# Attention's second product with the values as stationary operand and a transposed result, probabilities normalized first

## The chip, the core and the metric

The kernel runs on one core of a Trainium2 chip. The core has a matrix engine (TensorE, PE in the profile, with its weight loads as PEld), three engines for elementwise work (VectorE or DVE, ScalarE or ACT, GpSimd or POOL) and DMA queues, most of them issued from SyncE (SP). The metric is the device time of one execution in microseconds. Before the change three runs took 991.99, 993.06 and 994.40 us; the median is 993.06.

## The reference

Chunked attention feeds a dense feed-forward layer with squared ReLU, and that feeds a layer of eight experts, of which each token uses one:

```python
for c in range(nc):                       # chunks of 32 queries, 24 per sequence
    q_c = q[:, :, c_start:c_end]
    k_full = concat([mem_k, k[:, :, l_start:r_end]])      # 8 memory rows + 56 keys
    v_full = concat([mem_v, v[:, :, l_start:r_end]])
    scores = scale * q_c @ k_full.T
    a = exp(scores - max(scores))
    a = a / (sum(a) + 1e-09)
    out[:, :, c_start:c_end] = a @ v_full
x = out.transpose(0, 2, 1, 3).reshape(3072, 512)          # 8 heads of 64
x = relu(x @ w_in) ** 2 @ w_out                           # 512 -> 2048 -> 512
...                                                       # top-1 of 8 experts, 512 -> 1024 -> 512
```

All arrays are float32. Attention has 4 batches, 8 heads, 768 tokens and 64 numbers per head, so 3072 tokens in all.

## The kernel before

Tokens come in 24 units of 128, and two units form a block of 256. For each block b a class `Duo` does attention and a class `Block` does the dense layer; later, pairs and slots of tokens sorted by expert go through the experts.

A duo's steps: `scores_mm` multiplies queries by keys (64 products in float32, each with a stationary operand of 64 rows by 32 columns and 64 moving columns; a head pair `hp` has two heads in the two row halves, `par`, and four chunks `c` in four column groups). `scores_max`, `scores_sub` and `scores_exp` make e, with the queries of a unit on the partitions. `norm` sums e over the keys and takes the reciprocal r. `transpose_a` turns e with 8 transposes on TensorE and copies it to `at` on ScalarE. `av` multiplies `at` (stationary, 64 by 32) by the values (64 moving columns), again 64 products, and `av_scale` multiplies the result by r on VectorE into x. `transpose_x` turns x with 8 more transposes, and copies it as a rounded high part xh (ScalarE) and a remainder xl (VectorE), which are the moving operands of the dense layer. All these use one PSUM tile of two banks (tag "a", one buffer); the two row halves of `av` write to different banks (index `par`).

```python
nc.tensor.matmul(
    self.ps[ts][rows, par, n : n + 64],
    lhsT=left[t][half, hp, rows],
    rhs=right[t][half, hp, c, :],
```

The dense layer walks a list `seq` of (block, f), with 16 slices f of the hidden layer. Each step issues `mm1` (12 products of 256 columns and then relu and square on ScalarE and VectorE), then what `todo` planned for this step, then `mm2` of the step two before (6 products of 512 columns). Every engine takes its instructions in the order in which the program wrote them; a step of attention is put into that order by `plan_duo` with step numbers: scores and `norm` at s, `transpose_a` at t, `av` at v, `transpose_x` at x. Before: for duos 3 to 11 these are n+1, n+3, n+4 and n+6, where n is the first step of the block before (plus 3 for duo 4, plus 2 for duo 5). The loads of the next duo's keys and values are planned at x+1 and x+3, and its queries at x+2.

Duos 0 and 1 and the conversion of the first weight tiles (`split_w_...`, four VectorE passes and two ScalarE passes for each tile of w_in or w_out) are written out by hand ahead of that loop. Duo 0 goes through it unit by unit, u0 and u1. `keep_busy(n)` there issues n products whose result nobody reads (spin).

Of the kernel before, what the change touches and what calls it, by code (L numbers as in the profile page):

```python
# [8 lines left out]
F32 = mybir.dt.float32  # L9
# [5 lines left out]
ALU = mybir.AluOpType  # L15
AX = mybir.AxisListType

P = 128
# [8 lines left out]
NU = NT // P  # L27
UPS = 6
# [5 lines left out]
BOTH = (0, 1)  # L34
# [17 lines left out]
def chunk_attention_relu2_moe_top1_kernel(ctx: ExitStack, tc, qk, vv, qt, kv, w_in, w_out, wg, wexp, consts, out):  # L52
    nc = tc.nc
# [5 lines left out]
    ap_ = ctx.enter_context(tc.tile_pool(name="ap", bufs=2))  # L59
# [27 lines left out]

    class Duo:  # L90
        def __init__(self, b):
            self.b = b
            self.units = (2 * b, 2 * b + 1)
            self.first, self.q, self.k, self.v = {}, {}, {}, {}
            self.ps, self.mx, self.r = {}, {}, {}
            self.e = self.at = self.x = None


        def load_first(self, t):
# [87 lines left out]
        def norm(self, ts=BOTH):  # L187
            n = 8 * len(ts)
            sm = sp_.tile([P, n], F32, tag="sm", name=f"sm{self.b}_{ts[0]}")
            e = self.e[:, self.heads(ts)].rearrange("p a b k -> p (a b) k")  # L190
            nc.vector.tensor_reduce(out=sm, in_=e, axis=AX.X, op=ALU.add)
            nc.vector.tensor_scalar_add(sm, sm, EPS)
            self.r[ts] = sp_.tile([P, n // 2, 2], F32, tag="rs", name=f"rs{self.b}_{ts[0]}")
            nc.vector.reciprocal(self.r[ts].rearrange("p a b -> p (a b)"), sm)

        def transpose_a(self):
            self.transpose_a_mm()
# [15 lines left out]
            to = self.at[:, ts[0] : ts[-1] + 1].rearrange("p t a c -> p t (a c)")  # L213
            nc.scalar.copy(to, self.ps[ts][:, : len(ts)])

        def av(self):
            self.av_mm()
            self.av_scale()

        def av_mm(self, ts=BOTH, pool=ps_a, tag="a"):  # L220
            self.banks("psx", ts, pool, tag)
            self.products([self.at[:, 0], self.at[:, 1]], self.v, ts)

        def av_scale(self, ts=BOTH):
            if self.x is None:
                self.x = ap_.tile([P, 8, 2, 64], F32, tag="x", name=f"x{self.b}", bufs=1)
            nc.vector.tensor_tensor(
                self.x[:, self.heads(ts)].rearrange("p a b d -> p b a d"),
                self.by_half(ts),
                self.r[ts].rearrange("p a b -> p b a").unsqueeze(3).to_broadcast([P, 2, 4 * len(ts), 64]),  # L230
                op=ALU.mult,
            )

        def transpose_x(self):
            self.transpose_x_mm()
            self.transpose_x_copy()

        def transpose_x_mm(self, ts=BOTH, pool=ps_a, tag="a"):
            self.transposes("pst", self.x.rearrange("p a b d -> p (a b d)"), ts, pool, tag)

        def transpose_x_copy(self, ts=BOTH):
            self.transpose_x_hi(ts)
            self.transpose_x_lo(ts)

        def transpose_x_parts(self, ts):
            s = slice(ts[0] * P, ts[-1] * P + P)
            hi, lo = (x[:, :, s].rearrange("p k (t c) -> p t k c", c=P) for x in blocks[self.b].parts())
            return hi, lo, self.ps[ts][:, : len(ts)].rearrange("p t (k c) -> p t k c", c=P)

        def transpose_x_hi(self, ts=BOTH):  # L250
            hi, lo, ps = self.transpose_x_parts(ts)
            nc.scalar.copy(hi, ps)

        def transpose_x_lo(self, ts=BOTH):
            hi, lo, ps = self.transpose_x_parts(ts)
            nc.vector.tensor_tensor(lo, ps, hi.bitcast(F32), op=ALU.subtract)


# [522 lines left out]
    def plan(n, fn, *args):  # L781
        todo.setdefault(n, []).append((fn, args))

    def plan_duo(b, s, t, v, x):
        d = duos[b]
        plan(s, d.scores)
        plan(s, d.norm)
        plan(t, d.transpose_a)
        plan(v, d.av)
        plan(x, d.transpose_x)  # L790
        if b + 1 < NB:
            after = duos[b + 1]
            k0, q, k1 = (bits[15] + 1, s + 1, v + 1) if b == 2 else (x + 1, x + 2, x + 3)
            plan(k0, after.load_kv, 0)
            plan(q, after.load_q, 0)
            plan(q, after.load_q, 1)
            plan(k1, after.load_kv, 1)
# [3 lines left out]
    bits = dict(zip(range(3, 16), (2, 4, 6, 8, 10, 12, 14, 15, 17, 18, 20, 21, 23)))  # L801
# [13 lines left out]
    plan(bits[14] + 1, duos[2].load_kv, 1)  # L815
    plan(23, lambda: prepare())
    n = at[0, NF - 2]
    plan_duo(2, n - 3, n - 1, n, n + 2)
    for b in range(3, NB):
        n = at[b - 1, 0] + {4: 3, 5: 2}.get(b, 0)  # L820
        plan_duo(b, n + 1, n + 3, n + 4, n + 6)

    def plan_gate(b, n):
        bl = blocks[b]
# [5 lines left out]
    n = at[2, 7]  # L830
# [31 lines left out]
    for p in range(NP):  # L862
        n = at[NB + p, 0]
# [24 lines left out]
    n = at[NB, 0]  # L888
# [22 lines left out]
    with tc.manual_schedule():  # L911
        nc.gpsimd.memset(ones, 1.0)
        d0, d1 = duos[0], duos[1]
# [4 lines left out]
        def hold(tile_, until):  # L918
            nc.gpsimd.tensor_copy(tile_[0:1, 0:1], until)
# [12 lines left out]
        def keep_busy(n):  # L932
            for _ in range(n):
                nc.tensor.matmul(spin, lhsT=ones, rhs=ones.unsqueeze(1).to_broadcast([P, 4, P]), start=True, stop=True)
# [10 lines left out]
        d1.load_first_v()  # L945
        d0.scores_sub(u0)
        d0.scores_mm(u1, *other)
        d0.scores_exp(u0)
        d0.transpose_a_mm(u0)
        d0.transpose_a_copy(u0)  # L950
        keep_busy(3)
        d0.scores_max(u1)
        d0.scores_sub(u1)
        d0.scores_exp(u1)
        split_w_exp(*i0, a)
        d0.norm(u0)
        d0.av_mm(u0)
        d0.av_scale(u0)
        split_w_shift(*i0, a)
        split_w_or(*i0, a, steps=(0,))  # L960
        d0.transpose_a_mm(u1, *other)
        d0.transpose_a_copy(u1)
        keep_busy(3)
        d0.norm(u1)
        o0t = load_w(*o0, issue=False)
        hold(o0t.bitcast(F32), d0.r[u1][0:1, 0, 0:1])
        load_w(*o0)
        load_w(*i1)
        nc.sync.dma_start(cst[:, P:], consts[:, P:])
        d0.av_mm(u1, *other)  # L970
        d0.av_scale(u1)
        split_w_or(*i0, a, steps=(1,))
        d0.transpose_x_mm(u0)
        d0.transpose_x_hi(u0)
        keep_busy(4)
        d0.transpose_x_lo(u0)
        split_w_hi(*i0, a)
        split_w_lo(*i0, a)
        d0.transpose_x_mm(u1, *other)
        d0.transpose_x_copy(u1)  # L980
        d1.scores_mm()
        split_w_exp(*i0, b)
        b0.mm1_products(0)
        keep_busy(8)
# [3 lines left out]
        d1.scores_exp()  # L988
        split_w_shift(*i0, b)
        split_w_or(*i0, b)  # L990
        d1.transpose_a_mm()
        d1.transpose_a_copy()
        split_w_hi(*i0, b)
        d1.norm()
        split_w_lo(*i0, b)
        keep_busy(3)
        d1.av_mm()
        split_w_exp(*o0)
        b0.mm1_products(1)
        d1.av_scale()  # L1000
        split_w_shift(*o0)
        split_w_or(*o0, steps=(0,))
        d1.transpose_x_mm()
        d1.transpose_x_hi()
        keep_busy(4)
        d1.transpose_x_lo()
        split_w_or(*o0, steps=(1,))
        b0.relu(1)
        b1.mm1_products(0)
# [162 lines left out]
```

## Time and profile before

| | us |
|---|---|
| median of three runs | 993.06 |
| the profiled execution | 993.26 |
| its span, first to last instruction | 991.1 |
| TensorE busy | 966.1 (97%) |
| VectorE busy | 609.2 (61%) |
| ScalarE busy | 458.9 (46%) |
| GpSimd busy | 94.4 (10%) |

The span is what the profiler saw; the profiled execution's own time is 2.2 us longer. Busy time of TensorE counts matrix products whose ends are modelled, so it is not work at its peak. Duos 2 to 11 lie between 104 and 580 us of the span, where the dense layer runs; duos 0 and 1 lie in the first 33 us; the experts follow from about 660 us.

### The profile page before, as it was taken

To read this page: it belongs to the slowest core of one execution; us is meant where nothing else is said; L and a number is where in the kernel's file an instruction comes from. 1 tells how busy PE (TensorE), PEld (TensorE's weight loads), DVE (VectorE), ACT (ScalarE), POOL (GpSimd) and SP (SyncE) were. 2 spreads that over 40 slices of the span, in tenths; PEclk is the share of its full clock that TensorE was granted. 3 is DMA by queue.
4 is the path that set the end of the run, shared out by engine and by line. 5 is a ranking of instruction groups with operands and counts; after the bars stand their busy time and mean duration, and the time that the engine had idled before them with its cause. 6 is when DMAs were issued, how large, how long until landed. Compare 5 with 4: busy or idle time off the path is not lost. (4 is left out here: it accounts for less than half of the span.)

```text
span 991.1 us, 21589 instructions
## 1 busy us (share of the span) xinstructions
PE 966.1 (97%) x8973; PEld 856.3 (86%) x8973; DVE 609.2 (61%) x1133; ACT 458.9 (46%) x808; POOL 94.4 (10%) x92
## 2 busy tenths in 40 slices
PE   7899999989999999999999999999999999999996
PEld 4699898979999999999999998989899999888885
DVE  5989764434545454445453545647776666799995
ACT  3777433223333333333333333534454454688885
POOL 0000000100000000000000001101222221111111
PEclk9999999989999999999999999999999999999999
DMA  8456530220303030302021002663965666464531
GB/s 350 172 194 229 185 116 35 29 102 1 129 1 129 1 129 1 129 2 103 27 74 57 23 2 87 176 215 120 332 252 220 215 227 238 171 227 140 213 120 40
DMA packets 30855, 129.18 MB, mean 130 GB/s; under 512 B 8543, under 2 KB 9055, under 8 KB 18850
## 3 DMA queue, kind: packets, MB, share of 16 engines
q1 hardware_dynamic: 25506, 113.84, 32.0%
q0 software_dynamic: 5248, 13.92, 4.6%
q8 instruction: 72, 1.18, 0.5%
q14 instruction: 29, 0.24, 0.1%
HBM read 142.19 MB, written 13.61 MB: 157 GB/s over the span
## 5 line engine op out<-in xcount | busy, mean ns | idle before, releaser
L346 PE MATMUL ph<-xh,wi 128*128 128x256 f32 x1536 | 285.4, 283 | 3.0 <-ACT wi L305 1.0
L346 PEld LDWEIGHTS ph<-xh,wi 128*128 128x128 f32 x1536 | 252.0, 191 | 20.4 <-ACT wi L305 1.4
L346 PE MATMUL ph<-xl,wi 128*128 128x256 f32 x768 | 217.9, 284 | 4.1 <-issue 4.1
L356 ACT ACTIVATE r<-ph 128x256 f32<-128x256 f32 x192 | 73.3, 382 | 308.1 <-PE ph L346 288.8
L361 DVE TENSOR_TENSOR g<-r 128x256 f32<-128x256 f32 x168 | 70.9, 422 | 223.3 <-ACT r L356 222.2
L376 PE MATMUL py<-wo,gh 128*128 128x512 f32 x384 | 160.3, 417 | 0.0
L377 PE MATMUL py<-wo,gh 128*128 128x512 f32 x384 | 151.8, 395 | 0.0
L378 PE MATMUL py<-wo,gl 128*128 128x512 f32 x384 | 150.9, 393 | 0.0
L346 PEld LDWEIGHTS ph<-xl,wi 128*128 128x128 f32 x768 | 147.0, 191 | 4.3 <-issue 4.3
L613 DVE TENSOR_TENSOR x<-raw,x 128x1024 fp32r<-128x1024 f32 x88 | 103.1, 1222 | 6.7 <-ACT x L612 4.6
L365 DVE TENSOR_TENSOR gl<-g,gh 128x256 fp32r<-128x256 f32 x192 | 81.6, 425 | 24.4 <-ACT gh L363 2.4
L613 DVE TENSOR_TENSOR p<-raw,p 128x1024 fp32r<-128x1024 f32 x64 | 78.2, 1222 | 23.3 <-ACT p L612 22.3
L378 PEld LDWEIGHTS py<-wo,gl 128*128 128x128 f32 x384 | 72.7, 189 | 17.0
L612 ACT CAST x<-raw 128x1024 fp32r<-128x1024 f32 x88 | 87.2, 1055 | 0.0
L470 POOL DMA_INDIRECT listd<-ent,idx x24 | 24.2, 1009 | 630.1 <-DVE idx L468 570.8
L376 PEld LDWEIGHTS py<-wo,gh 128*128 128x128 f32 x384 | 73.1, 190 | 12.8 <-issue 2.2
L363 ACT ACTIVATE gh<-r 128x256 fp32r<-128x256 f32 x192 | 79.8, 416 | 5.3
L377 PEld LDWEIGHTS py<-wo,gh 128*128 128x128 f32 x384 | 73.3, 191 | 8.3
L612 ACT CAST p<-raw 128x1024 fp32r<-128x1024 f32 x64 | 66.6, 1040 | 0.0
L759 PE MATMUL po<-x,ht 128*128 128x512 f32 x264 | 65.5, 397 | 0.6 <-DVE ht L749 0.6
L759 PEld LDWEIGHTS po<-x,ht 128*128 128x128 f32 x264 | 48.1, 188 | 10.2 <-DVE ht L749 1.0
L629 POOL DMA_INDIRECT out<-o,slots x27 | 35.5, 1316 | 216.0 <-DVE o L623 94.5
(217 smaller groups left out, 1356.9 us busy)
## 6 DMA issues: line engine op xcount, KB each, us to landing
raw<-in_wexp SPq DMA_DIRECT2D x82, 1024.0 KB
kv<-in_kv SPq DMA_DIRECT2D x20, 1024.0 KB
raw_o<-in_w_out SPq DMA_DIRECT2D x8, 1024.0 KB
raw_i<-in_w_in SPq DMA_DIRECT2D x7, 1024.0 KB
ydram<-y SPq DMA_DIRECT2D x24, 256.0 KB
q<-in_qt SPq DMA_DIRECT2D x20, 256.0 KB
qk<-in_qk SPq DMA_DIRECT2D x4, 768.0 KB
v<-in_vv SPq DMA_DIRECT2D x2, 1024.0 KB
```

Of the source, the lines that this page charges most:

```text
L346: nc.tensor.matmul(ph, lhsT=w_in_part(w, f, k), rhs=x[:, k, :], start=(n == 0), stop=(n == 11))
L356: nc.scalar.activation(r, ph, ACTF.Relu, scale=WSCALE)
L361: nc.vector.tensor_tensor(g, r, r, op=ALU.mult)
L363: nc.scalar.activation(gh, r, ACTF.Square)
L365: nc.vector.tensor_tensor(gl, g, gh.bitcast(F32), op=ALU.subtract)
L376: nc.tensor.matmul(self.y[t], lhsT=gh[:, s], rhs=w_out_part(wh, f), start=(f == 0), stop=False)
L377: nc.tensor.matmul(self.y[t], lhsT=gh[:, s], rhs=w_out_part(wl, f), start=False, stop=False)
L378: nc.tensor.matmul(self.y[t], lhsT=gl[:, s], rhs=w_out_part(wh, f), start=False, stop=(f == NF - 1))
L612: nc.scalar.copy(w[:, 0], t)
L613: nc.vector.tensor_tensor(w[:, 1], t, w[:, 0].bitcast(F32), op=ALU.subtract)
L629: nc.gpsimd.indirect_dma_start(out=out, out_offset=bass.IndirectOffsetOnAxis(ap=slots[:, c, 0:1].bitcast(U32), axis=0), in_=self.y[t], in_ ...
L759: nc.tensor.matmul(self.po, lhsT=self.ht[:, part, f, :], rhs=w[:, wp, j * D : j * D + D], start=(f == 0 and part == 0 and wp == 0), stop=( ...
```

## The change

`norm` now also multiplies e by r, ahead of `transpose_a`. `av_mm` takes the values of a chunk and head as stationary operand (64 rows by 64 columns) and 32 columns of `at` as moving operand, so that its result already has the head's numbers on the partitions and the tokens along the columns, which is the form that the dense layer reads. `av_scale`, the tile x and the 8 transposes of x are gone; xh and xl are taken from the product's PSUM tile. There are four places in the array for a 64 by 64 operand. A product reads row half `par` and writes partition half `par ^ t`, with t the unit in the duo; for the second unit the host therefore swaps the two heads of each pair (`in_turn`). The bank of the result is now the unit `i`.

The plan has `norm` at its own step m, and no x: for duos 3 to 11 scores n+1, norm n+2, `transpose_a` n+5, `av` n+6. The order by hand at the start is rewritten.

```diff
     def norm(self, ts=BOTH):
...
+            self.r[ts] = sp_.tile([P, n], F32, tag="rs", name=f"rs{self.b}_{ts[0]}")
+            nc.vector.reciprocal(self.r[ts], sm)
+            nc.vector.tensor_tensor(e, e, self.r[ts].unsqueeze(2).to_broadcast([P, n, 64]), op=ALU.mult)
...
+        def av(self, ts=BOTH, pool=ps_a, tag="a"):
+            self.av_mm(ts, pool, tag)
+            self.x_hi(ts)
+            self.x_lo(ts)
 
         def av_mm(self, ts=BOTH, pool=ps_a, tag="a"):
             self.banks("psx", ts, pool, tag)
-            self.products([self.at[:, 0], self.at[:, 1]], self.v, ts)
-
-        def av_scale(self, ts=BOTH):
...
-        def transpose_x_mm(self, ts=BOTH, pool=ps_a, tag="a"):
-            self.transposes("pst", self.x.rearrange("p a b d -> p (a b d)"), ts, pool, tag)
...
+            for hp in range(4):
+                for c in range(4):
+                    for i, t in enumerate(ts):
+                        for par in range(2):
+                            half = slice(64 * par, 64 * par + 64)
+                            to = 64 * (par ^ t)
+                            n = P * hp + 32 * c
+                            nc.tensor.matmul(
+                                self.ps[ts][to : to + 64, i, n : n + 32],
+                                lhsT=self.v[t][half, hp, c, :],
+                                rhs=self.at[half, t, hp, 32 * c : 32 * c + 32],
...
-    def plan_duo(b, s, t, v, x):
+    def plan_duo(b, s, m, t, v):
         d = duos[b]
         plan(s, d.scores)
-        plan(s, d.norm)
+        plan(m, d.norm)
         plan(t, d.transpose_a)
         plan(v, d.av)
-        plan(x, d.transpose_x)
...
-            k0, q, k1 = (bits[15] + 1, s + 1, v + 1) if b == 2 else (x + 1, x + 2, x + 3)
+            k0, q, k1 = (bits[15] + 1, s + 1, v + 1) if b == 2 else (v + 1, v + 2, v + 3)
...
-    plan_duo(2, n - 3, n - 1, n, n + 2)
+    plan_duo(2, n - 3, n - 3, n, n + 1)
...
-        plan_duo(b, n + 1, n + 3, n + 4, n + 6)
+        plan_duo(b, n + 1, n + 2, n + 5, n + 6)
...
         split_w_shift(*i0, b)
         split_w_or(*i0, b)
+        d1.norm()
+        split_w_hi(*i0, b)
         d1.transpose_a_mm()
         d1.transpose_a_copy()
-        split_w_hi(*i0, b)
-        d1.norm()
         split_w_lo(*i0, b)
-        keep_busy(3)
-        d1.av_mm()
         split_w_exp(*o0)
         b0.mm1_products(1)
-        d1.av_scale()
+        d1.av_mm()
+        d1.x_hi()
+        d1.x_lo()
         split_w_shift(*o0)
         split_w_or(*o0, steps=(0,))
-        d1.transpose_x_mm()
-        d1.transpose_x_hi()
         keep_busy(4)
-        d1.transpose_x_lo()
         split_w_or(*o0, steps=(1,))
         b0.relu(1)
         b1.mm1_products(0)
```

In the part of the hand-written order that is left out, for duo 0, `keep_busy(4)` stands ahead of `scores_exp(u0)` and `d1.scores_mm()` is followed by `keep_busy(4)` and then by the first products of the dense layer, where it was followed by these products at once.

VectorE at duo 1 (e_443, psx_0_478, xl_572 are this duo's; ws_o, wo and raw_o belong to the first tile of w_out, wi to the first of w_in), before:

```order
L191 TENSOR_REDUCE sm_0_469<-e_443 128x16
L192 TENSOR_SCALAR sm_0_469<-sm_0_469 128x16
L194 RECIPROCAL rs_0_472<-sm_0_469 128x16
L310 TENSOR_TENSOR wi_344<-ws_i_232,wi_344 128x512
L227 TENSOR_TENSOR x_558<-psx_0_478,rs_0_472 128x2x8x64
L285 TENSOR_SCALAR ws_o_543<-ws_o_543 128x1024
L292 SCALAR_TENSOR_TENSOR ws_o_543<-raw_o_290,ws_o_543 128x1024
L256 TENSOR_TENSOR xl_572<-pst_0_562,xh_571 128x2x4x128
L296 SCALAR_TENSOR_TENSOR ws_o_543<-raw_o_290,ws_o_543 128x1024
L365 TENSOR_TENSOR gl_1_586<-g_1_582,gh_1_584 128x256
```

and of the change (e_436, psx_0_484 and xl_550 are the duo's):

```order
L192 TENSOR_REDUCE sm_0_450<-e_436 128x16
L193 TENSOR_SCALAR sm_0_450<-sm_0_450 128x16
L195 RECIPROCAL rs_0_453<-sm_0_450 128x16
L196 TENSOR_TENSOR e_436<-e_436,rs_0_453 128x1024
L307 TENSOR_TENSOR wi_409<-ws_i_242,wi_409 128x512
L253 TENSOR_TENSOR xl_550<-psx_0_484,xh_549 128x2x4x128
L282 TENSOR_SCALAR ws_o_469<-ws_o_469 128x1024
L289 SCALAR_TENSOR_TENSOR ws_o_469<-raw_o_286,ws_o_469 128x1024
L293 SCALAR_TENSOR_TENSOR ws_o_469<-raw_o_286,ws_o_469 128x1024
L362 TENSOR_TENSOR gl_1_566<-g_1_562,gh_1_564 128x256
```

Before, two passes over the weight tile (L285, L292) stand between the scaling of x and the remainder xl; now xl stands ahead of all three passes over that tile, and behind the multiplication of e only one short pass (wi) is ahead of it.

TensorE at the second product of duo 4 (kv_2125 and kv_2207 hold the values of its two units), before, first the product and then, two steps later, the transposes of x:

```order
L135 MATMUL psx_0_2786<-kv_2125,at_2757 32x64 x32
L135 MATMUL psx_0_2786<-kv_2207,at_2757 32x64 x32
L376 MATMUL py_2564<-wo_790,gh_5_2717 128x512
...
L346 MATMUL ph_9_2886<-xl_2095,wi_982 128x256
L205 MATMUL pst_0_2907<-cst,x_2851 128x128 x8
L376 MATMUL py_2564<-wo_918,gh_7_2782 128x512
```

and of the change, the last four rows of the product and what follows:

```order
L234 MATMUL psx_0_2801<-at_2772,kv_2085 64x32 x2
L234 MATMUL psx_0_2801<-at_2772,kv_2167 64x32 x2
L234 MATMUL psx_0_2801<-at_2772,kv_2085 64x32 x2
L234 MATMUL psx_0_2801<-at_2772,kv_2167 64x32 x2
L373 MATMUL py_2524<-wo_898,gh_7_2732 128x512
L374 MATMUL py_2524<-wo_898,gh_7_2732 128x512
```

The product still counts 64, now with the two units in turn, and stands two steps later; the row of 8 transposes is gone.

## Rows read from the trace of the kernel before

**Rows 1.** The page: engines (busy us, share, instructions); the TensorE instruction queue (packets, MB).
```profile
PE 966.1 (97%) x8973; PEld 856.3 (86%) x8973; DVE 609.2 (61%) x1133; ACT 458.9 (46%) x808; POOL 94.4 (10%) x92
...
q8 instruction: 72, 1.18, 0.5%
```
**Rows 2.** Waits of TensorE: what for, us in total, times, longest.
```profile
PE ph L346 <- issue: 4.1, 1, 4.1
...
PE ph L346 <- ACT wi L305: 1.0, 1, 1.0
...
PE ph L346 <- DVE wi L310: 0.9, 1, 0.9
```
**Rows 3.** Timeline of TensorE at duo 11: start us, length us, instruction, count.
```profile
569.68 0.28 PE L346 MATMUL ph<-xl,wi 128*128 128x256 f32 x1
569.89 1.48 PE L135 MATMUL psx<-kv,at 64*32 64x64 f32 x128
571.31 0.50 PE L376 MATMUL py<-wo,gh 128*128 128x512 f32 x1
571.64 0.39 PE L377 MATMUL py<-wo,gh 128*128 128x512 f32 x1
571.87 0.40 PE L378 MATMUL py<-wo,gl 128*128 128x512 f32 x1
...
576.93 0.28 PE L346 MATMUL ph<-xl,wi 128*128 128x256 f32 x1
577.05 1.04 PE L205 MATMUL pst<-cst,x 128*128 128x128 f32 x8
577.84 0.47 PE L376 MATMUL py<-wo,gh 128*128 128x512 f32 x1
578.16 0.39 PE L377 MATMUL py<-wo,gh 128*128 128x512 f32 x1
```
**Rows 4.** Instructions that write psx: count, shortest, median and longest in ns.
```profile
L135 PE MATMUL psx<-kv,at x1280: 212/216/240, 117.0 to 571.2; 64*32 64x64 f32 x183
```
**Rows 5.** Timeline of VectorE, duo 1 and the first weight tiles; idle time before in brackets.
```profile
22.80 0.42 DVE L365 TENSOR_TENSOR gl<-g,gh 128x256 fp32r<-128x256 f32 x1 [0.25 <-ACT gh L363]
...
24.93 1.21 DVE L191 TENSOR_REDUCE sm<-e 128x16 f32<-128x1024 f32 x1
...
27.73 1.21 DVE L227 TENSOR_TENSOR x<-psx,rs 128x1024 f32<-128x1024 f32 x1
...
31.38 1.23 DVE L256 TENSOR_TENSOR xl<-pst,xh 128x1024 fp32r<-128x1024 f32 x1 [0.53 <-ACT xh L252]
...
33.66 0.42 DVE L365 TENSOR_TENSOR gl<-g,gh 128x256 fp32r<-128x256 f32 x1
...
39.98 1.23 DVE L310 TENSOR_TENSOR wi<-ws_i,wi 128x1024 fp32r<-128x1024 f32 x1 [0.17 <-ACT wi L305]
```
**Rows 6.** Timeline of ScalarE at duo 1.
```profile
30.34 1.01 ACT L252 CAST xh<-pst 128x1024 fp32r<-128x1024 f32 x1 [2.82 <-PE pst L205]
```
**Rows 7.** Timeline of TensorE: work behind its waits.
```profile
18.96 1.00 PE L135 MATMUL pss<-qk 64*32 64x64 f32 x76 [1.77 <-issue]
...
32.00 1.04 PE L934 MATMUL spin<-ones 128*128 128x512 bf16 x4 [1.69 <-issue]
...
41.27 0.38 PE L346 MATMUL ph<-xh,wi 128*128 128x256 f32 x1 [0.88 <-DVE wi L310]
...
204.43 0.58 PE L346 MATMUL ph<-xl,wi 128*128 128x256 f32 x1 [4.12 <-issue]
```
**Rows 8.** Stretches: us, busy us by engine, granted clock of TensorE (1.00 full), DMA share, GB/s.
```profile
202.00:206.00 4.00, 1.57 (x6) 1.47 (x7) 1.06 (x3) 0.30 (x1) 0.00 (x0) 0.55 0.33 119
206.00:210.00 4.00, 4.00 (x19) 3.52 (x18) 0.85 (x2) 0.50 (x2) 0.00 (x0) 0.60 0.01 4
```
**Rows 9.** DMA from 201.9 to 203.2 us by queue: packets, MB, share of 16 engines.
```profile
q8 instruction: 1, 0.02, 5.3%
```
**Rows 10.** Timeline of SyncE's queue: issue of a load of keys and values.
```profile
192.62 0.40 SPq L123 DMA_DIRECT2D kv<-in_kv  x1
```

More of the change, by code (lines that the diff above doesn't have):

```diff
@@ L95, in __init__ @@
             self.ps, self.mx, self.r = {}, {}, {}
-            self.e = self.at = self.x = None
+            self.e = self.at = None
         def load_first(self, t):
@@ L192, in norm @@
             nc.vector.tensor_scalar_add(sm, sm, EPS)
-            self.r[ts] = sp_.tile([P, n // 2, 2], F32, tag="rs", name=f"rs{self.b}_{ts[0]}")
-            nc.vector.reciprocal(self.r[ts].rearrange("p a b -> p (a b)"), sm)
+            self.r[ts] = sp_.tile([P, n], F32, tag="rs", name=f"rs{self.b}_{ts[0]}")
+            nc.vector.reciprocal(self.r[ts], sm)
+            nc.vector.tensor_tensor(e, e, self.r[ts].unsqueeze(2).to_broadcast([P, n, 64]), op=ALU.mult)
         def transpose_a(self):
@@ L214, in transpose_a_copy, with x_parts @@
             nc.scalar.copy(to, self.ps[ts][:, : len(ts)])
-        def av(self):
-            self.av_mm()
-            self.av_scale()
+        def av(self, ts=BOTH, pool=ps_a, tag="a"):
+            self.av_mm(ts, pool, tag)
+            self.x_hi(ts)
+            self.x_lo(ts)
         def av_mm(self, ts=BOTH, pool=ps_a, tag="a"):
             self.banks("psx", ts, pool, tag)
-            self.products([self.at[:, 0], self.at[:, 1]], self.v, ts)
-        def av_scale(self, ts=BOTH):
[L225 to L236, printed above, removed]
-        def transpose_x_mm(self, ts=BOTH, pool=ps_a, tag="a"):
-            self.transposes("pst", self.x.rearrange("p a b d -> p (a b d)"), ts, pool, tag)
[L241 to L245, printed above, removed]
+            for hp in range(4):
[9 more added lines that the diff above has]
+                                rhs=self.at[half, t, hp, 32 * c : 32 * c + 32],
+                                start=True,
+                                stop=True,
+                            )
+        def x_parts(self, ts):
             s = slice(ts[0] * P, ts[-1] * P + P)
@@ L248, in transpose_x_parts, with x_hi, x_lo @@
             return hi, lo, self.ps[ts][:, : len(ts)].rearrange("p t (k c) -> p t k c", c=P)
-        def transpose_x_hi(self, ts=BOTH):
-            hi, lo, ps = self.transpose_x_parts(ts)
+        def x_hi(self, ts=BOTH):
+            hi, lo, ps = self.x_parts(ts)
             nc.scalar.copy(hi, ps)
-        def transpose_x_lo(self, ts=BOTH):
-            hi, lo, ps = self.transpose_x_parts(ts)
+        def x_lo(self, ts=BOTH):
+            hi, lo, ps = self.x_parts(ts)
             nc.vector.tensor_tensor(lo, ps, hi.bitcast(F32), op=ALU.subtract)
@@ L947, in chunk_attention_relu2_moe_top1_kernel @@
         d0.scores_mm(u1, *other)
+        keep_busy(4)
         d0.scores_exp(u0)
+        d0.scores_max(u1)
+        d0.norm(u0)
         d0.transpose_a_mm(u0)
         d0.transpose_a_copy(u0)
-        keep_busy(3)
-        d0.scores_max(u1)
         d0.scores_sub(u1)
         d0.scores_exp(u1)
+        keep_busy(3)
         split_w_exp(*i0, a)
-        d0.norm(u0)
         d0.av_mm(u0)
[L958 to L963, printed above, removed]
+        d0.x_hi(u0)
         d0.norm(u1)
         o0t = load_w(*o0, issue=False)
-        hold(o0t.bitcast(F32), d0.r[u1][0:1, 0, 0:1])
+        hold(o0t.bitcast(F32), d0.r[u1][0:1, 0:1])
         load_w(*o0)
@@ L969, in chunk_attention_relu2_moe_top1_kernel @@
         nc.sync.dma_start(cst[:, P:], consts[:, P:])
+        d0.x_lo(u0)
+        keep_busy(3)
+        d0.transpose_a_mm(u1, *other)
+        d0.transpose_a_copy(u1)
+        split_w_shift(*i0, a)
+        split_w_or(*i0, a)
         d0.av_mm(u1, *other)
[L971 to L974, printed above, removed]
+        d0.x_hi(u1)
+        d1.scores_mm()
         keep_busy(4)
-        d0.transpose_x_lo(u0)
+        d0.x_lo(u1)
         split_w_hi(*i0, a)
         split_w_lo(*i0, a)
-        d0.transpose_x_mm(u1, *other)
-        d0.transpose_x_copy(u1)
-        d1.scores_mm()
         split_w_exp(*i0, b)
@@ L990, in chunk_attention_relu2_moe_top1_kernel @@
         split_w_or(*i0, b)
+        d1.norm()
+        split_w_hi(*i0, b)
         d1.transpose_a_mm()
         d1.transpose_a_copy()
-        split_w_hi(*i0, b)
-        d1.norm()
         split_w_lo(*i0, b)
-        keep_busy(3)
-        d1.av_mm()
         split_w_exp(*o0)
         b0.mm1_products(1)
-        d1.av_scale()
+        d1.av_mm()
+        d1.x_hi()
+        d1.x_lo()
         split_w_shift(*o0)
         split_w_or(*o0, steps=(0,))
-        d1.transpose_x_mm()
-        d1.transpose_x_hi()
         keep_busy(4)
-        d1.transpose_x_lo()
         split_w_or(*o0, steps=(1,))
@@ L1107, with in_turn @@
     B, H, S, DH = q.shape
-    qt = q.reshape(B, 4, 2, UPS, P, DH).transpose(0, 3, 2, 5, 1, 4).reshape(NU, P, 4, P)
+    def in_turn(x):
+        x = x.reshape(NU, 2, 64, *x.shape[4:]).copy()
+        x[1::2] = x[1::2, ::-1]
+        return x.reshape(NU, P, *x.shape[3:])
+    qt = in_turn(q.reshape(B, 4, 2, UPS, P, DH).transpose(0, 3, 2, 5, 1, 4))
     def windows(x, mem):
@@ L1120 @@
         [
-            kwn.transpose(0, 3, 2, 6, 1, 4, 5).reshape(NU, P, 4, 4, 64),
-            vwn.transpose(0, 3, 2, 5, 1, 4, 6).reshape(NU, P, 4, 4, 64),
+            in_turn(kwn.transpose(0, 3, 2, 6, 1, 4, 5)),
+            in_turn(vwn.transpose(0, 3, 2, 5, 1, 4, 6)),
         ],
```

## The prediction

> **What bounds the kernel now.** I began with the page: TensorE is busy for 966.1 of 991.1 us, VectorE for 609.2 [rows 1]. So a saving counts where it shortens TensorE's own queue, and only there. The second view was TensorE's waits: they are few, one of 4.1 us put down to "issue", which means that no engine and no data transfer held it, and two of about 1 us for converted weights (wi) from ScalarE and VectorE [rows 2]. The third was the timeline. In the loop TensorE goes from product to product without a gap, so a step of attention costs what it pushes the next product back [rows 3]. In the first 45 us it is different: VectorE works almost without a pause on duo 1 and the first weight tiles, and TensorE waits for what it delivers [rows 5, 7]. Two stretches thus obey two rules, and I price the change in each apart.
>
> **The loop, duos 2 to 11.** The transposes of x are removed. In duo 11 they begin at 577.05, where the next product would have begun (0.12 us after the one at 576.93), and that product begins at 577.84, 0.79 us later. The one behind it follows after 0.32 where 0.23 is usual [rows 3], which adds 0.09. So 0.88 us for each duo, and 10 duos give -8.8 us. The pattern is the same in all ten.
>
> The second product keeps its 64 instructions, in the trace 128 records since each float32 product runs twice. Before, it takes from 569.89 to 571.31, 1.42 us or 11 ns a record [rows 3]. Eight places of the array share them, so one place spends about 90 ns on a record. Of this the 64 moving columns are one part and the load of 32 stationary columns is another that hides under it. Now there are four places, the moving columns halve and the stationary ones double. What a load costs when nothing hides it can be read twice: the longest psx product, the first, takes 240 ns against 216, 24 ns for 32 columns [rows 4]; and the first dense product behind the small ones takes 0.50 against 0.40 us, some 0.1 us for 128 columns [rows 3]. That is about 0.8 ns a column, so a load of 64 columns is an estimated 50 ns. If each place loads while it multiplies, four places deliver a record each 12.5 to 15 ns, and 128 records take 1.6 to 1.9 us. The low end of the cost is nothing: the run stays at 1.42, if the instructions' supply and not the array sets its pace. Less than that I exclude, since neither the instructions nor moving columns for each place in the array become fewer. The high end is that loads and products share the array by two and not by four: 128 times 27 ns, 3.4 us, +2.0. I take +0.5, by the nearer rows, and 10 duos give +5.0 us.
>
> VectorE and ScalarE do as much as before in the loop: a multiplication of 1024 elements (1.21 us [rows 5]) changes its place and its source. It is hidden: `norm` is planned three steps ahead of the transposes, some 8 us, and VectorE is far from full there. Without that cover each duo would cost TensorE up to those 1.2 us. The later `transpose_a` and `av` only use the steps that `transpose_x` leaves. On SP the loads of keys stay at the same steps (v+1 is what x+1 was); on POOL nothing moves in the loop. Both units' values come free at the product's end and not one after the other, within the same 2 us, and nobody waits for that buffer in this stretch. Together the loop gives -3.8 us.
>
> **The start.** In duo 0 chains get longer, but TensorE is held in duo 1's scores until 18.96 in any case [rows 7], and I count nothing there. In duo 1 the chain counts. Four idle products now stand ahead of the first dense products (four last about 0.9 us [rows 7]), so gl at 22.80 [rows 5], which comes from these, moves to 23.7, and all behind it on VectorE too: the sum to 25.8. From the sum to the scaling 2.80 us passed, with a short wi pass of about 0.55 that now comes later; the multiplication starts at 28.05 and ends at 29.25. Then come 8 transposes (0.8), twelve dense products of 0.12 (1.45), the second product (1.5 to 2.0, with its tail), xh on ScalarE (1.01 [rows 6]). The remainder xl, at 31.38 before, can start at 34.7. Meanwhile VectorE has only the wi pass and then stands idle for some 4.5 us, since the three passes over the first tile of w_out are queued behind xl. Before, two of them (from 27.73 plus scaling to the wait of 0.53 ahead of 31.38, 2.0 us) ran during that wait. So the gl that began 2.28 us behind xl, at 33.66, now begins 4.28 behind it, at 39.0: 5.3 us late. From there VectorE hardly pauses before wi at 39.98, for which TensorE waits at 41.27 [rows 5, 7], so TensorE is as late there and never gets it back, being full afterwards. The transposes saved in duos 0 and 1 lie inside these waits. I take +5.0, between 3.5 (no tail at the second product, some idle time swallowed) and 6.5.
>
> On SP the load behind the next tile waits for the same passes and moves with them; POOL's copy that lets the first w_out load go follows duo 0's reciprocal, which moves by under 1 us.
>
> **The stall at 200 us.** This is the largest single item. TensorE stops for 4.12 us until 204.43 without waiting for anything [rows 7]. Its instructions arrive in 72 packets for 17,946 instructions, about 250 each [rows 1]. I counted in the order of instructions (four for a small float32 product, two for others): the three long stops [rows 7] stand at instruction 706, 1218 and 4547, which leave 194, 194 and 195 when divided by 256. So these are ends of blocks of 256 whose successor has not come. Before the restart one instruction packet arrives, after 201.9 [rows 9], behind a load of keys and values of 1 MB issued at 192.62 [rows 10]. Then the clock is granted at about half until 209.2 (0.55 and 0.60 as means [rows 8]): 4.8 us at half speed cost 2.4. The stop costs 6.5 us in all. By my count the change removes 59 instructions ahead of this place (64 for the transposes of duos 0 to 3, less a few idle products and waits), so the block ends 59 instructions later behind duo 4's scores. A step of the dense layer is 36 instructions and 2.85 us, so TensorE reaches the end 4.4 us later, when the packet that came late before has just come. I take -6.5; the bounds are nothing, if the three timed runs had no such stop or the packet is as late again, and -6.5.
>
> **Sum.** On the profiled execution: 993.26 - 8.8 + 5.0 + 5.0 - 6.5 = 988.0. The median lies 0.2 below that execution, so 987.8.
>
> **Rivals.**
> First, the stall stays, or was never in the timed runs. Then -8.8 + 5.0 + 5.0 = +1.2, so 994.3. For it: it was one event in one profile. Against it: the three runs lie within 2.4 us of each other and of the profiled one, and a cost of 6.5 that comes and goes would show. Chance 0.28.
>
> Second, the second product costs no more than before, as its pace is set by the supply of instructions. Then 5.0 less: 982.8 without the stall, 989.3 with it. For it: 90 ns for each place are more than a load or the moving columns seem to need. Chance 0.17.
>
> Third, on the slower side: the four places don't work side by side. Before, row halves write to different banks; now the two heads of one unit write to one bank. If such a pair takes turns, the run takes up to 3.4 us and costs 10 to 20 us over ten duos in place of 5: 993 to 1003 without the stall, 999 to 1009 with it. It decides as soon as the run in the loop lasts over 2.9 us with the stall gone, or 2.2 with it. No row of before shows such a pair. Chance 0.17.
> The Trainium skill speaks for this rival: "TensorEngine Tiling (Array Packing)", section "Gotcha 1: PSUM Pressure", says that different row tiles cannot access the same PSUM bank at the same time. By that the forecast becomes the third rival; no trace of before tests it.
>
> **How the numbers follow.** The forecast has 0.38, with a range of its own of 984.5 to 991 from the bounds of the start and a few us on the product. From 982 to 998.5 the range leaves out the lower edge of the second rival and most of the third, under 0.2 together. A measurement of this kernel tells a change of about 0.2%, 2 us, from none. Faster by more: 0.37 of the forecast, 0.16 of the second rival, 0.01 of the others, 0.54. Within 0.2%: 0.01 of the forecast and of the second rival, 0.14 of the first, 0.04 of the third, 0.20. Slower: 0.13 of the first, 0.13 of the third, 0.26.
>
> **What the profile after would show.** The psx run in the loop tells the second term: 1.4 us, 1.6 to 2.0, or over 2.5. No row pst. VectorE idle for over 3 us ahead of duo 1's xl, and wi some 5 us later than 39.98. No wait "issue" of several us between 110 and 600 us, and a granted clock of 1.00 there. The forecast is wrong if a new stop of that sort appears at another block's end, if the start loses much more or less than 5 us, or if the product's run doubles.

## The result: 0.6 to 0.9% slower

The changed kernel takes 1001.85 us (median of 4 runs, 999.31 to 1002.35), the kernel before beside it 992.52 (988.5 to 994.4): a ratio of 1.0091, 95% interval [1.0067, 1.0115]. On another chip it was 1001.05 against 995.18, 1.0056 [1.0040, 1.0073]. The forecast was 987.8, within 982.0 to 998.5.

The page of the changed kernel, engines first, then the clock granted to TensorE in 40 slices of 25 us:

```profile
PE 973.0 (98%) x8878; PEld 861.6 (86%) x8878; DVE 608.9 (61%) x1133; ACT 458.4 (46%) x808; POOL 97.5 (10%) x92
...
PEclk7899999999999999999999999999999999999999
```

TensorE has 95 records fewer than in [rows 1] and is busy 6.9 us longer. The first slice (0.7) says where to look.

**The loop** is as forecast. Duo 11 of the changed kernel, timeline of TensorE, and its instructions that write psx (shortest, median, longest in ns):

```profile
582.14 0.28 PE L343 MATMUL ph<-xl,wi 128*128 128x256 f32 x1
582.36 2.07 PE L234 MATMUL psx<-at,kv 64*64 64x32 f32 x128
584.35 0.50 PE L373 MATMUL py<-wo,gh 128*128 128x512 f32 x1
584.69 0.39 PE L374 MATMUL py<-wo,gh 128*128 128x512 f32 x1
```

```profile
L234 PEld LDWEIGHTS psx<-at,kv x1280: 129/135/135, 132.2 to 584.2; 64*64 64x64 f32 x183
L234 PE MATMUL psx<-at,kv x1280: 219/219/240, 132.2 to 584.2; 64*64 64x32 f32 x183
```

The second product holds TensorE from 582.36 to 584.35, 1.99 us against 1.42 [rows 3], and no pst is left.

**The start** is not. Timeline of TensorE, changed kernel (release of a wait in brackets):

```profile
11.70 0.63 PE L207 MATMUL psa<-cst,e 128*128 128x128 f32 x4 [1.83 <-DVE e L196]
...
13.01 3.50 PE L234 MATMUL psx<-at,v 64*64 64x32 f32 x64
...
19.43 3.62 PE L234 MATMUL psx<-at,v 64*64 64x32 f32 x64 [0.68 <-ACT at L216]
22.99 2.06 PE L136 MATMUL pss<-qk 64*32 64x64 f32 x128
...
34.79 1.94 PE L207 MATMUL psa<-cst,e 128*128 128x128 f32 x8 [4.71 <-DVE e L196]
...
39.23 2.62 PE L234 MATMUL psx<-at,v 64*64 64x32 f32 x128
...
54.83 0.39 PE L343 MATMUL ph<-xh,wi 128*128 128x256 f32 x1 [0.61 <-DVE wi L307]
```

The last row answers to 41.27 in [rows 7]: 13.6 us later, where I had 5.3. (TensorE gets some of it back before duo 2, whose scores start 12.0 us later: before, it was busy for 48.25 of the 50 us from 60 to 110, now for all of them.) VectorE's rows name the chain, the end of duo 1's normalization and the remainder of x:

```profile
33.42 1.23 DVE L196 TENSOR_TENSOR e<-e,rs 128x1024 f32<-128x1024 f32 x1
34.56 0.68 DVE L307 TENSOR_TENSOR wi<-ws_i,wi 128x512 fp32r<-128x512 f32 x1
42.97 1.22 DVE L253 TENSOR_TENSOR xl<-psx,xh 128x1024 fp32r<-128x1024 f32 x1 [7.72 <-ACT xh L249]
```

VectorE is idle for 7.72 us ahead of xl (0.53 before [rows 5]; I had said some 4.5). And the granted clock, by stretches (columns as in [rows 8]), first two of the kernel before, then the changed one:

```profile
12.00:20.00 8.00, 4.67 (x206) 3.55 (x206) 5.27 (x10) 2.94 (x6) 0.17 (x1) 1.00 1.02 422
20.00:28.00 8.00, 7.01 (x161) 4.85 (x162) 7.51 (x11) 4.67 (x7) 1.23 (x5) 1.00 0.72 269
```

```profile
0.00:12.00 12.00, 9.15 (x151) 4.02 (x152) 4.50 (x9) 1.91 (x2) 0.59 (x6) 1.00 0.82 304
12.00:20.00 8.00, 7.30 (x90) 5.46 (x87) 4.16 (x8) 2.84 (x5) 0.70 (x1) 0.57 1.02 413
20.00:28.00 8.00, 8.00 (x201) 6.84 (x200) 3.74 (x4) 1.70 (x3) 1.23 (x5) 0.57 0.54 220
28.00:36.00 8.00, 3.29 (x17) 2.07 (x17) 5.53 (x9) 2.67 (x5) 0.00 (x0) 0.85 0.35 131
36.00:44.00 8.00, 7.32 (x150) 6.12 (x148) 1.03 (x1) 4.11 (x7) 0.00 (x0) 0.72 0.01 2
```

From 12 to 28 us TensorE ran close to its lower level of 1.2 GHz (0.57 of 2.4). In the kernel before the clock was 1.00 there.

**The stall at 200 us** changed its place, into duo 4's scores. Its rows in the first profile of the changed kernel, and then in the second one, from another chip:

```profile
208.95 0.31 PE L136 MATMUL pss<-kv,q 64*32 64x64 f32 x4 [0.33 <-issue]
209.70 0.54 PE L136 MATMUL pss<-kv,q 64*32 64x64 f32 x28 [0.44 <-issue]
210.82 0.95 PE L136 MATMUL pss<-kv,q 64*32 64x64 f32 x49 [0.58 <-issue]
```

```profile
211.88 1.54 PE L136 MATMUL pss<-kv,q 64*32 64x64 f32 x43 [2.78 <-issue]
```

Cutting every profile at the starts of the scores of duos 2, 5 and 11 (rows pss of TensorE's timeline; us) separates the three parts:

| profile | start to duo 2 | duo 2 to 5 (stall) | duo 5 to 11 (loop) | duo 11 to end |
|---|---|---|---|---|
| before | 104.60 | 147.45 | 306.86 | 432.2 |
| before, again | 104.72 | 144.84 | 306.82 | 434.0 |
| changed | 116.61 | 143.93 | 305.22 | 431.7 |
| changed, again | 116.72 | 146.29 | 305.28 | 434.3 |
| old start | 105.61 | 141.95 | 305.42 | 431.5 |
| new start, old loop | 112.45 | 142.77 | 308.50 | 432.5 |
| xl behind the passes | 111.67 | 146.45 | 305.24 | 433.5 |
| old duo 0 | 111.38 | 143.46 | 305.22 | 433.4 |
| old duo 1 | 110.90 | 143.18 | 305.68 | 434.1 |
| clock held | 112.03 | 147.20 | 305.35 | 433.8 |
| loads held (start and loop of before) | 106.16 | 142.12 | 306.84 | 433.8 |
| wide | 111.26 | 142.55 | 305.37 | |
| old start, loads held | 105.99 | 141.70 | 305.21 | 432.1 |
| old duo 1, clock held | 108.27 | 143.76 | 305.22 | 433.1 |

The last stretch moves by 2.6 us between executions of one kernel, so differences of that size in a whole span mean nothing. The old start by itself lies between 104.60 and 106.16 in five profiles. The 308.50 of the new start with the old loop contains another stop put down to issue, 1.26 us at 474.51.

### The profile page after: what moved, and what is told of

Same layout as the page of the kernel before. It is cut to its first block, busy times and chain, and to the rows that moved or that the text cites. A ratio compares the mean times of both kernels' runs of the same rounds, so it can differ in the third digit from the quotient of the medians.

```text
span 997.5 us, 21398 instructions
## 1 busy us (share of the span) xinstructions
PE 973.0 (98%) x8878; PEld 861.6 (86%) x8878; DVE 608.9 (61%) x1133; ACT 458.4 (46%) x808; POOL 97.5 (10%) x92
## 5 line engine op out<-in xcount | busy, mean ns | idle before, releaser
L373 PEld LDWEIGHTS py<-wo,gh 128*128 128x128 f32 x384 | 73.1, 190 | 14.1 <-issue 2.4
L756 PEld LDWEIGHTS po<-x,ht 128*128 128x128 f32 x264 | 48.1, 188 | 10.2 <-DVE ht L746 1.0
```

Of the source, the lines that this page charges most:

```text
L373: nc.tensor.matmul(self.y[t], lhsT=gh[:, s], rhs=w_out_part(wh, f), start=(f == 0), stop=False)
L756: nc.tensor.matmul(self.po, lhsT=self.ht[:, part, f, :], rhs=w[:, wp, j * D : j * D + D], start=(f == 0 and part == 0 and wp == 0), stop=( ...
```

## Experiments

**1. Old start, new loop.** Duos 0 and 1 and the order around them as before, the changed methods (here with names of their own) from duo 2 on; heads are swapped in every second unit from unit 5 on.

```diff
-        plan(s, d.norm)
+        plan(m, d.norm_first)
         plan(t, d.transpose_a)
-        plan(v, d.av)
-        plan(x, d.transpose_x)
+        plan(v, d.av_turned)
```

> Duos 0 and 1 as before (their order by hand too), the change in the loop alone (duos 2 to 11). Theory A (the start carries the loss, 13.6 us at the first wait for wi): the loop gains 0.31 us a duo, so 989.4 us with a stop such as that at 200 us, some 983 without. Rival B (the loop or what follows it loses, the start's delay is taken up later): about 1000 us, as the whole change.

989.09 us, ratio 0.9953 [0.9931, 0.9974]. wi's wait ends at 42.23. The version with the old start gains, so the loss is in the start. The time is the one that I had put down for a kernel with the stop at 200 us, but this profile has none: 141.95 us from duo 2 to 5, and only two waits of 0.39 and 0.42 us in duo 4's scores. So the 989.4 was met in part by luck, and part of the gain is the missing stop and not the loop.

**2. New start, old loop**, the reverse.

> The change in duos 0 and 1 alone, with its order by hand; duos 2 to 11 as before. Theory A: 13.6 us more than before, 1006 us with the stop at 200 us, 999.6 without. Rival B: within 2 us of before, 991 to 994 us.

999.08, ratio 1.0051 [1.0032, 1.0070]. The start alone loses, though this profile too has no long stop at 200 us (142.77). But the same instructions come to wi sooner than in the changed kernel, and the unit products take 2.06 instead of 3.50 us:

```profile
12.56 2.06 PE L279 MATMUL psx<-at,v 64*64 64x32 f32 x64
...
50.65 0.39 PE L375 MATMUL ph<-xh,wi 128*128 128x256 f32 x1 [0.57 <-DVE wi L339]
```

The granted clock was 1.00 up to 28 us here. So the clock is a suspect beside the order.

**3. xl behind the passes.** In the changed kernel the passes over the first tile of w_out go ahead of duo 1's xl.

```diff
         d1.x_hi()
-        d1.x_lo()
         split_w_shift(*o0)
-        split_w_or(*o0, steps=(0,))
+        split_w_or(*o0)
+        d1.x_lo()
         keep_busy(4)
-        split_w_or(*o0, steps=(1,))
```

> The whole change, with the three VectorE passes over the first w_out tile moved ahead of duo 1's remainder xl, whose wait of 7.7 us they can fill. Theory A: the passes' 3.1 us leave the path, 998.7 us, and TensorE's waits for wo (1.4 and 0.8 us) go. Rival B: no change within 1 us, 1001.9 us.

996.89, ratio 1.0039 [1.0020, 1.0058], which overlaps the changed kernel's second interval. The waits for wo are gone, and wi's wait ends at 49.87, 4.96 us earlier than in the changed kernel's first profile:

```profile
41.78 0.38 PE L343 MATMUL ph<-xl,wi 128*128 128x256 f32 x1 [0.76 <-DVE xl L253]
...
49.87 0.38 PE L343 MATMUL ph<-xh,wi 128*128 128x256 f32 x1 [0.87 <-DVE wi L307]
```

From the first product with xl to this wait 8.09 us pass; in both profiles of the changed kernel, and in runs 2 and 10 with the unaltered new start, it is 10.57 or 10.58. So the passes in VectorE's gap bring 2.5 us, near the 3.1 of theory A. The other 2.47 us are xl's own: it comes earlier (41.78 against 44.25), with a clock of 1.00 from 12 to 20 us and 0.79 from 20 to 28.

**4. The kernel before, one look.**

> The kernel before, unchanged, for a second trace. If the stop of 4.12 us at 200.31 belongs to the kernel's own alignment of instruction blocks and loads, it is there again within 1 us of that place, with the clock at half behind it; if it was a chance event, the trace has none there and the span is 985 to 988 us.

992.54. The stop comes again, 3.1 us at the same instruction, this time without the half clock behind it: the stop stands in both profiles, its price differs.

**5. The changed kernel again, on the chip of runs 6 to 8.**

> The changed kernel unaltered, beside the three that follow, as their base. Both theories: slower than before by 0.5 to 0.9% (998 to 1002 us where before takes 993). Theory A (the chain of the start, VectorE and ScalarE in turn, sets the loss): the first wait for wi ends at about 50.5 us, as in the kernel with the new start and the old loop (50.65), and about 4 us later only if TensorE's clock falls to half from 13 us on, as it did in the first profile (54.83). Theory B (the clock sets most of the loss): it ends at 54 to 55 each time.

Ratio 1.0056 as given above. wi's wait ends at 54.88 and the stretches from 12 to 28 us have a clock of 0.58 and 0.56. Of its six runs three have a mean clock of 0.982 to 0.987 and three 0.989 to 0.990; the latter take 999.7 to 1000.4 us, the former 1001.7 to 1004.4. The profiled execution is the slowest of the six, so its rows are the worse sort.

**6. Old duo 0, new duo 1 and loop.**

> Duo 0 as before the change, duo 1 and the loop as after it. My prediction's step for the start puts the whole loss into duo 1 and nothing into duo 0: by it this kernel equals the changed one (within 1 us). Theory A, that each unit of duo 0 has only two places for its second product and a longer chain, so that duo 1's scores come some 4 us later (18.96 before, 22.99 after): wi's wait ends about 4 us earlier than in the changed kernel, near 46.5, and the time is 4 to 5 us below it. Rival: the changed duo 1 alone lets the clock fall, then less than 2 us is gained.

995.74, ratio 1.0012 [0.9998, 1.0026].

```profile
49.60 0.39 PE L380 MATMUL ph<-xh,wi 128*128 128x256 f32 x1 [0.58 <-DVE wi L344]
```

Against run 1 duo 1's change costs 0.59%, 5.8 us, and 5.8 us in the first column of the table: close to the 5.0 that I had put there, with a clock of 0.58 from 28 to 36 us in it. wi's wait ends 5.3 us earlier than in run 5, as the time does, but not near the 46.5 that I had written.

**7. New duo 0, old duo 1, new loop.**

> Duo 0 as after the change, duo 1 as before it, the loop as after it. By my prediction's step (duo 1's chain costs 5.0, duo 0 nothing): as the kernel with both duos old (989.1 where before takes 993.6, ratio 0.9953). Theory A: duo 0 costs 4 us by itself, wi's wait ends near 46 (42.23 with both old) and the ratio to before is about 0.9995. If the two parts add, this one and the kernel with the old duo 0 lose together what the changed one loses against both old.

991.05, ratio 0.9962 [0.9945, 0.9980]: 0.9 us over run 1, within the intervals. Theory A's 4 us fall. But its profiled execution shows 5.3 us in the first column, with the half clock of the changed kernel:

```profile
13.04 3.40 PE L284 MATMUL psx<-at,v 64*64 64x32 f32 x64
...
47.62 0.58 PE L380 MATMUL ph<-xh,wi 128*128 128x256 f32 x1 [0.87 <-DVE wi L344]
```

That execution was one of the three slowest of twelve (995.5 to 996.3 at a clock of 0.988 to 0.990); the other nine lie between 988.2 and 992.6 at 0.993 to 0.996. By these executions duo 0's share goes with the clock; only one of them has a profile.

**8. Clock held.** The changed kernel with idle products in TensorE's waits.

```diff
         d0.norm(u0)
+        keep_busy(7)
         d0.transpose_a_mm(u0)
...
         split_w_or(*i0, a)
+        keep_busy(2)
         d0.av_mm(u1, *other)
...
-        keep_busy(8)
+        keep_busy(27)
         d1.scores_max()
...
+        keep_busy(5)
         b0.mm2(0)
```

> The changed kernel with 33 more idle products on TensorE, in its waits of the start: 7 ahead of duo 0's first transposes, 2 ahead of the second unit's second product, 19 ahead of duo 1's transposes, 5 ahead of the first product of the dense layer's second half. Theory B (clock): no stretch at half clock before 45 us, unit psx 2.06 us each in place of 3.5, wi's wait 4 us earlier than in the changed kernel beside it if that has the half clock from 13 us on, and 1.5 to 2 us earlier if it has it only around duo 1's transposes and second product; the time as much shorter. Theory A alone (VectorE and ScalarE set the chain, TensorE's part of it is small): less than 1 us.

999.2, ratio 1.0038 [1.0024, 1.0052]. The start behaves as expected, clock 1.00 up to 36 us and wi 4.6 us earlier than in run 5:

```profile
12.00:20.00 8.00, 6.79 (x189) 5.34 (x187) 5.10 (x10) 4.19 (x8) 0.70 (x1) 1.00 1.02 424
20.00:28.00 8.00, 7.31 (x113) 4.62 (x114) 5.42 (x8) 2.59 (x6) 1.76 (x5) 1.00 0.53 217
```

```profile
50.24 0.38 PE L343 MATMUL ph<-xh,wi 128*128 128x256 f32 x1 [0.87 <-DVE wi L307]
...
211.43 0.37 PE L343 MATMUL ph<-xl,wi 128*128 128x256 f32 x1 [4.42 <-issue]
```

VectorE starts duo 1's multiplication at 29.20 and xl at 36.18, 4.2 and 6.8 us earlier than in the changed kernel's first profile. Part of this is lost again behind xl: from TensorE's first product with xl to wi 12.78 us pass here and not 10.58. The median fell by 1.8 us only, and the intervals touch, so the timed runs don't show a gain. The second row names one cost in this profile: a stall of 4.4 us stands again, with a clock of 0.50 from 211 to 215 us.

**9. Loads held**, on the kernel before: does the block of instructions come late because of the loads?

```diff
             kvt = kvp.tile([P, 2, 4, 4, 64], F32, tag="kv", name=f"kv{u}")
+            if self.b == 5 and t == 0:
+                nc.gpsimd.tensor_copy(kvt[0:1, 0, 0, 0, 0:1], duos[4].at[0:1, 0, 0, 0:1])
             nc.sync.dma_start(kvt, kv[u - EARLY])
```

> The kernel before, with one element copied by GpSimd from duo 4's transposed probabilities into duo 5's tile of keys and values ahead of its load, so that this load and the queries behind it start some 10 us later (near 207 instead of 192.6 and 197.2) and nothing of them is under way when TensorE comes to the end of its block of 256 instructions at 200 us. My reading of the stall (the next block of instructions comes late because it stands behind this load): the wait of 3 to 4 us put down to issue, and the 2 to 2.4 us at issue around duo 4's scores, fall below 1 us together, and the time from duo 2's scores to duo 5's is 142.5 to 143.5 us where it was 147.45 and 144.84 in two profiles; the median 2 to 4 us lower. Rival (the block is late by itself, or for another load): the waits stay near 5 us in all and the time is as before.

990.18, ratio 0.9961 [0.9948, 0.9975]. The loads now start at 208.5 (SyncE's queue), and of the stop two short waits are left on TensorE:

```profile
208.54 0.33 SPq L125 DMA_DIRECT2D kv<-in_kv  x1
208.98 0.85 SPq L118 DMA_DIRECT2D q<-in_qt  x2
```

```profile
199.39 0.33 PE L137 MATMUL pss<-kv,q 64*32 64x64 f32 x6 [0.35 <-issue]
200.15 0.37 PE L137 MATMUL pss<-kv,q 64*32 64x64 f32 x10 [0.42 <-issue]
```

Duo 2 to 5 takes 142.12 (expected 142.5 to 143.5). TensorE's instructions are the same (8973 records). The instruction packet that lands at 201.6 to 202.0 in the two profiles of before, with the loads under way, lands at 197.2 to 197.4 here, ahead of them. So the cause is that the instructions stood behind the loads. Where the block ends must matter as well: in run 1, with the loads where they were, the packet is as late (202.0), and yet there is no long stop.

**10. Wide second product**, 64 moving columns in place of 32 in the loop.

```diff
                             n = P * hp + 32 * c
+                            m, w = (32 * c, 32) if self.b < 2 else (32 * min(c, 2), 64)
+                            n = P * hp + m
                             nc.tensor.matmul(
-                                self.ps[ts][to : to + 64, i, n : n + 32],
+                                self.ps[ts][to : to + 64, i, n : n + w],
                                 lhsT=self.v[t][half, hp, c, :],
-                                rhs=self.at[half, t, hp, 32 * c : 32 * c + 32],
+                                rhs=self.at[half, t, hp, m : m + w],
```

> The changed kernel with 64 moving columns instead of 32 in each instruction of duo 2 to 11's second product, overlapping, so that its output is not the reference's from there. The stationary side (64 columns) and the four places stay. If the loading of 64 stationary columns, or the places, set the 1.99 us of the run (theory L): it stays at 1.95 to 2.1. If in each place load and product follow each other (theory M; from 62 ns a record and place now and 89 ns before, by columns, 0.36 ns for a stationary and 1.21 for a moving one): some 100 ns a record, 3.2 us. If the number of instructions sets it: 1.99 as well, so this run tells M from the other two.

```profile
575.86 2.10 PE L236 MATMUL psx<-at,kv 64*64 64x64 f32 x128
577.89 0.50 PE L375 MATMUL py<-wo,gh 128*128 128x512 f32 x1
```

2.03 us where 1.99 stood: theory M (3.2) falls, and from 32 to 64 moving columns are nearly free. The 64 instructions before were done in 1.42, so their number isn't it either. What is left is some 62 ns a record on each of four places; whether that is the load of 64 stationary columns or another fixed cost of a product, no run separates. The time of its single run, 991.4, isn't compared, since what its tokens are routed to at the end isn't the same. Its start, unaltered, ran at clock 1.00 to 28 us and reached wi at 49.47.

**11. Old start, new loop, loads held**: runs 1 and 9 together.

> The start as before the change, the changed loop from duo 2 on (the fastest so far, 0.9953 of before), and duo 5's loads held as in the kernel with held loads. If loads are what delays the instructions: no wait at issue over 0.5 us around duo 4's scores, the ratio 0.991 to 0.995. If not: 0.9953.

987.16, ratio 0.9941 [0.9926, 0.9957], the fastest version found. Against run 9, which differs in the loop alone, it gains 3.0 us, though the two intervals still meet at their ends.

**12. Old duo 1, clock held in duo 0.**

> Duo 0 and the loop as after the change, duo 1 as before it, with 9 more idle products in duo 0 (7 ahead of the first transposes, 2 ahead of the second unit's second product). The same without them has a ratio of 0.9962 to before, with executions of two sorts: clock 0.988 to 0.990 and 995 to 996 us, clock 0.993 to 0.996 and 988 to 993 us; both duos old has 0.9953. If the clock makes duo 0's share: only the second sort is left, unit psx 2.06 us each, wi's wait near 43.5, the ratio 0.995 or a little less. If duo 0's longer chain by itself costs some us: no change of the ratio (0.996 to 0.997) though the clock is held.

991.36, ratio 0.9988 [0.9968, 1.0007]: not the 0.995 expected, and no better than run 7. The clock in its profile is 1.00 up to 44 us, the unit products take 2.06 us, and still wi comes 2.6 us later than in run 1:

```profile
44.87 0.39 PE L380 MATMUL ph<-xh,wi 128*128 128x256 f32 x1 [0.87 <-DVE wi L344]
```

This delay isn't duo 0's chain: VectorE scales duo 1's x at 28.81, in run 1 at 28.77. (Run 1 had a clock of 0.93 and 0.85 from 12 to 28 us; before, at full clock, it was 27.73 [rows 5], so chain and idle products cost some 1.1 us.) The delay comes behind that, where a stop put down to issue falls between the second and the third transpose of x:

```profile
33.09 0.88 PE L205 MATMUL pst<-cst,x 128*128 128x128 f32 x6 [2.47 <-issue]
```

In run 1 such a stop (1.74 us, until 32.96) falls behind all eight transposes, where xl waits for nothing more from TensorE. So xl starts 2.7 us later here (35.04 against 32.31), which is the difference in the first column too (108.27 against 105.61): it is the price of where a block of instructions ends. How much of it the timed runs of run 7 paid stays open: the intervals of runs 7 and 12 meet only at their ends.

## Why the prediction was wrong

**The loop: right.** I had -8.8 + 5.0. One duo's period fell from 52.08 to 51.81 us, 0.27 in place of 0.38, and runs 9 and 11 differ by 3.0 us where I had 3.8. The product cost 0.57 a duo where I took 0.5. The second rival (no cost) and the third (3.4 us) fall, since the run lasts 1.99 us. The Trainium skill, "TensorEngine Tiling (Array Packing)", section "Gotcha 1: PSUM Pressure", says that different row tiles can't access one bank at the same time. The 3.4 us that I had made of this did not come; shorter turns than I had priced aren't excluded, since a unit of duo 0 alone, two places and one bank, takes 2.06 us for half the records.

**The start: the failed step.** "I take +5.0, between 3.5 and 6.5." The first column of the table gives +12.0 in both profiles of the changed kernel. The chain was the one I wrote down, and where the clock stayed at 1.00 up to 28 us the same start costs 6.6 us (run 10) and 7.8 (run 2) over before, a little above my range, with a clock of 0.79 and 0.58 from 28 to 36 us still in it. What failed is that every duration in it came from rows at full clock. The transposes (0.8) took 1.60, until 36.39; the twelve dense products (1.45) 2.84, until 39.23; the second product 2.55 to the next instruction at 41.78. The multiplication ended at 34.65 and not at 29.25, as duo 1's scores ended at 25 and not at 20. In the sum xl is 8.3 us later than my 34.7, and wi 8.2 later than the forecast of 46.6. Run 8 tests this: with the clock held the multiplication starts at 29.20 where I had 28.05, and xl at 36.18 where I had 34.7. So of the 8.3 us at xl 6.8 go with the clock and 1.5 are mine. From xl to wi the changed kernel takes 10.58 us, as forecast (8.60 before [rows 5] and 2.0 for the passes behind xl; run 3, without them there, takes 8.09).

"I count nothing there" for duo 0 failed too: the fall of the clock begins in its chain. Each unit of duo 0 has two places for its second product, since both heads' values stand in one row half each and only two of the four places are used, and one bank: 2.06 us at full clock, where a whole duo takes 1.99. And the multiplication stands ahead of the transposes, for which TensorE waits 1.8 us at 9.9. That wait came ahead of the fall at 12 us in each profile with the fall (runs 5, 7 and the first), but runs 2, 3 and 10 had it too and kept the clock, to 28 us or, in run 3, to 20. With the wait filled (runs 8 and 12) no profile shows the fall. That the wait brings it on is thus likely, not shown. Why it comes in some executions and not in others isn't settled.

**The stall: the other failed step.** "I take -6.5." The stop did move, but into duo 4's scores and not behind them, and the packet was as late again: 1.35 and 2.78 us of waits in two profiles, with half clock behind. Against the undisturbed 141.70 (run 11) the changed kernel lost 2.2 and 4.6 us from duo 2 to 5, the kernel before 5.3 and 2.7 against 142.12 (run 9). On average of two and two 0.6 us were saved, not 6.5, and no more can be said of so few: this is the first rival, to which I gave 0.28. The cause I named was right (run 9), but moving the end by 59 instructions doesn't take it out of the loads' way here; with the old start (run 1) the end falls where no long stop comes. The 59 itself was not counted in a run. I also took one execution with the half clock for the rule; run 4 shows a stop without it. (59 instructions at 36 in 2.85 us are 4.7 us and not 4.4, which changes nothing.)

**The sum.** In the table, two profiles against two, the start gives +12.0, duo 2 to 5 -1.0 (stall -0.6, loop -0.4), duo 5 to 11 -1.6 and the rest -0.1: +9.3. The timed medians rose by 9.3 us on one chip and 5.9 on the other. That the first is the same number is chance: the profiled spans differ by 6.4 us on the one chip and by 12.2 between the second pair. In the timed runs the start can't be taken apart so well: runs 1 and 5 differ by 1.03%, some 10.2 us, but run 5's profile also has 4.3 us more from duo 2 to 5. Against the forecast of 987.8 the measured 1001.85 is 14.1 us more; by the table 7.0 of that are the start and 5.9 the stall.

## What to carry to other kernels

In a start where engines wait for each other in turn, durations from rows at full clock are a lower bound: look for new waits that the change gives TensorE, and price the chain at both levels of the clock. Before counting a stall as removed, ask what would make it go, and test that cause by itself: holding one load and the queries behind it back brought 3.5 us, about as much as the whole loop of the change (3.0). A change in the number of instructions also moves where the blocks end: in run 12's profile that alone made 2.7 us. A change that helps the steady loop can be kept out of the start.

## What the hardware showed unexpectedly

- Small products on four places: with 64 stationary columns the run of 128 records takes 1.99 us whether 32 or 64 columns move through (2.03). With two places, 64 records take 2.06.
- A stop of TensorE, waiting for nothing that the profile shows, of 4.12 and 3.10 us in two profiles, went down to waits of 0.35 and 0.42 us when 1.5 MB of loads were started 12 to 16 us later (run 9); the instruction packet then landed over 4 us earlier.
- One and the same start ran at a clock of 0.57 from 12 to 28 us in some executions and at 1.00 in others, which goes with about 5 us at duo 2's scores (116.61 and 116.72 against 111.26).
